# Folding w3 with w_out as plain fp32 products instead of three products of high and low parts

## The chip, the core and the metric

The kernel runs on one core of a Trainium2 chip. The metric is the device time of one execution in microseconds (us); lower is better. The time of the kernel before is 1035.65 us, the median of three runs (1032.55 to 1035.98).

## What is computed

Attention with a memory term over 4 batches of 8 heads, 576 tokens and 64 dimensions, then two feed-forward blocks over the 2304 tokens:

```python
x = attention(q, k, v, M_prev, z_prev, beta)    # (2304, 512)
a = x @ w1                                      # (2304, 1024)
b = x @ w2
h = a * b @ w3                                  # w3: (1024, 1024)
x = h @ w_out                                   # w_out: (1024, 512)
h = x @ w_in                                    # (2304, 2048)
out = (h - tanh(h)) @ w_out2                    # (2304, 512)
```

The weights of both feed-forward blocks arrive as 64-bit floats. Nothing stands between w3 and w_out, so the kernel multiplies the two once (the fold) and uses the product WF = w3 @ w_out, 1024 by 512.

## The kernel before, in words

**Stages.** Attention runs first, as 80 units (16 pairs of heads, five blocks of queries each); beside it, as background, the weights are decoded and folded. Then come six groups of 384 tokens through the first block (`ab` and `x` products), then six through the second (`h` and `o`).

**A unit of attention.** TensorE computes scores for two heads (`sc`), VectorE takes the negated maximum (L337), ScalarE the exponential with its sum (L346), VectorE the reciprocal of the sum (L355, L356), GpSimd multiplies (L363), TensorE transposes (`t`, L395 to L406), ScalarE or VectorE copies (L374, L376), and in two units of five TensorE forms the product with v (`o<-g,v`). The scores and these products are plain fp32 matmuls.

**Decoding.** A `Decoder` turns 64-bit tiles of 128 x 512 into fp32 in steps, handed out one at a time. `dec_ops` is one tile: an absolute value on ScalarE (L74) and a clamp on VectorE (L75), step one; a shift (L77), step two; the low bits (L81), step three; the sign (L84), step four. With `whole` the last writes its result into the place that `dst()` names and ends there. Without it there is a step five: GpSimd copies the result into an fp32r tile, the high part (L96), and subtracts that from the result, the low part (L99). A product of two such pairs is three fp32r matmuls: high by high, high by low, low by high.

**The fold.** `fold_work` decodes 8 tiles of w_out (`FO`, into the places z0 to z3, wa0, wb0, wa1, wb1 that later hold other weights) and 16 of w3 (`zs`; eight column blocks f, two halves of the contraction), one tile in work at a time (DW = 1), three loads ahead. After each w3 tile it issues the matmuls of that f and half, four blocks of three, into a PSUM tile `fo`; the first half is copied to a partial sum (L254), the second added to it (L257) and split into WF's high and low part (L259, L260).

**Pacing.** The background is a generator. ST = 8 steps of it are taken before the first unit. After each unit `BG` (units below MB = 40) or `BG2` (from 40 on) is added to a credit, and each whole credit takes one step; a block of fold matmuls takes none. Behind the fold the background does one group of the memory term (17 steps) and decodes four weight tiles of the first block (NE = 4), at three steps a round, 51 in all; what is left when the 80 units end is run at once. Within these bounds the compiler's scheduler orders each engine's instructions. SP's queue carries all loads.

Of the kernel before, what the change touches and what calls it, by code (L numbers as in the profile page):

```python
# [11 lines left out]
F32 = mybir.dt.float32  # L12
F32R = mybir.dt.float32r
BF16 = mybir.dt.bfloat16
U32 = mybir.dt.uint32
# [17 lines left out]
def block_kernel(ctx, tc, qk, qt, vt, mp, zp_d, beta, w1, w2, w3t, wo, wi, wo2, ident_d, mask_d, out):  # L33
# [8 lines left out]
    zp = ctx.enter_context(tc.tile_pool(name="zp", bufs=1, side="right"))  # L42
# [12 lines left out]
    def wslot(pool, tag, dt=F32R):  # L55
        return pool.tile([128, 2, 512], dt, tag=tag, name=tag if dt == F32R else tag + "p")
# [85 lines left out]
    def mm(o, lhsT, rhs, start, stop):  # L142
        return PE.matmul(o, lhsT, rhs, start=start, stop=stop).ins  # L143
# [14 lines left out]
    DW = 1  # L158
# [5 lines left out]
    OP, FL = 5, "V"  # L164
    SN, XP, MR = 2, (), 0
    TH = (("V", 0), ("A", 0))
    NE, EM, BG = 4, 1, 2.13
    BG2, MB = 2.09, 40
    MS, FS, FS5 = 4, 3, 6
    CPA = (0, 1, 3, 4)  # L170

# [6 lines left out]
    ap1, ap2, apr, ap3, ap4 = [apl[x] for x in "12r34"]  # L178
# [20 lines left out]
    def slot(tag, dt=F32R):  # L199
        return wslot(wl[0] if tag in ("wa7", "wb7") else zp if tag[0] == "z" else wfp if tag[:2] == "wf" else wp if int(tag[2]) < NE // 2 else wq[0], tag, dt)  # L200
# [4 lines left out]
    otags = ztags[:4] + etags[:4]  # L205
    FO, fv = {}, {}

    def fold_o_item(j):
        def dst():
            FO[j] = slot(otags[j])  # L210
            return FO[j][:, 0], FO[j][:, 1]

        return wo[j * 128:j * 128 + 128], dst

    def fold_item(f, half):
        def dst():
            t = wslot(ap1, "zs")
            fv[f, half] = t
            return t[:, 0], t[:, 1]

        r = slice(512 * half, 512 * half + 512)
        return w3t[r, f * 128:f * 128 + 128].rearrange("(k p) c -> p k c", p=128), dst

    def fold_work(psum):
        seq = [("o", j) for j in range(4)]
        for f in range(8):
            if f >= OP:
                seq += [("o", 4 + f - OP)] if 4 + f - OP < 8 else []
            seq.append((f, 0))
        seq += [("o", j) for j in range(12 - OP, 8)]  # L230
        for f in range(8):
            seq += [("x", i) for i, x in enumerate(XP) if x == f]
            seq.append((f, 1))
        make = {"o": fold_o_item, "x": lambda i: w_items[i]}
        dec = Decoder([make[k[0]](k[1]) if k[0] in make else fold_item(*k) for k in seq], DW, 3)
        part = {}
        for half in range(2):
            for f in range(8):
                while dec.done <= seq.index((f, half)) or half and dec.done <= seq.index(("o", 7)):
                    dec.step()  # L240
                    yield
                acc = psum()
                t = fv.pop((f, half))
                for j in range(4):
                    o = FO[4 * half + j]
                    c = slice(128 * j, 128 * j + 128)
                    mm(acc, t[:, 0, c], o[:, 0], j == 0, False)
                    mm(acc, t[:, 0, c], o[:, 1], False, False)
                    mm(acc, t[:, 1, c], o[:, 0], False, j == 3)
                    if j % FG == FG - 1:  # L250
                        yield 1
                if half == 0:
                    part[f] = wslot(wfp, f"wf{f}", F32)
                    AC.activation(out=part[f][:, 0], in_=acc, func=AF.Copy)  # L254
                else:
                    s = ap1.tile([128, 512], F32, tag=f"s{f % SN}", name="s")
                    DV.tensor_tensor(out=s, in0=acc, in1=part[f][:, 0], op=ALU.add)  # L257
                    WF[f] = wslot(wfp, f"wf{f}")
                    AC.activation(out=WF[f][:, 0], in_=s, func=AF.Copy)  # L259
                    (DV if FL == "V" else PO).tensor_tensor(out=WF[f][:, 1], in0=s, in1=WF[f][:, 0].bitcast(F32),  # L260
                                                            op=ALU.subtract)
                    yield 2

    if True:
# [271 lines left out]
        def early():  # L536
            a, b, end = None, chain(*[mem_group(g) for g in range(EM)]), object()
            ps["t"] = lambda: psT.tile([128, 512], F32, tag="t", name="mt")
            ps["o"] = lambda: psA.tile([128, 512], F32, tag="o", name="mo")
            for x in fold_work(lambda: psA.tile([128, 512], F32, tag="o", name="fo")):  # L540
                if x == 2:
                    if not mem_t:
                        mem_setup()
                    for _ in range(MR):
                        if b and next(b, end) is end:
                            b = None
                        yield
                else:
                    yield x
            if not mem_t:  # L550
                mem_setup()
            a = early_w()
            while a or b:
                if b and next(b, end) is end:
                    b = None
                yield
                for _ in range(2):
                    if a and next(a, end) is end:
                        a = None
                    yield  # L560
# [69 lines left out]
        def ab_pe(xl, f):  # L630
            o = []
            for W in (W1, W2):
                p = psb.tile([128, 512], F32, tag="ab", name="ab")
                for k in range(4):
                    c = slice(k * 128, k * 128 + 128)
                    mm(p[:, 0:N], W[f][:, 0, c], xl[0][:, k], k == 0, False)
                    mm(p[:, 0:N], W[f][:, 0, c], xl[1][:, k], False, False)
                    mm(p[:, 0:N], W[f][:, 1, c], xl[0][:, k], False, k == 3)
                o.append(p)
            return o  # L640
# [104 lines left out]
        for g in range(6):  # L745
            for f in range(8):
                wd.until(2 * f + 2)
                o = ab_pe(xl, f)
# [169 lines left out]
def build(nc, arrays):  # L918
    args = []
    for name, a in arrays.items():  # L920
        args.append(nc.dram_tensor(f"in_{name}", a.shape, mybir.dt.from_np(a.dtype), kind="ExternalInput").ap())
    o = nc.dram_tensor("out_0", (_N, 512), F32, kind="ExternalOutput").ap()
    with tile.TileContext(nc, schedule_with_timeline_sim=True) as tc:
        block_kernel(tc, *args, o)
# [40 lines left out]
```

## Time and profile before

| | |
|---|---|
| median of three runs | 1035.65 us (1032.55 to 1035.98) |
| profiled execution, its own time | 1031.13 us |
| its span | 1029.3 us |
| TensorE busy over the span | 982.1 us, 95% |
| VectorE | 752.1 us, 73% |
| ScalarE | 592.9 us, 58% |
| GpSimd | 360.5 us, 35% |
| mean granted TensorE clock | 0.991 |

PE is TensorE's matmul side, PEld its weight loads, DVE VectorE, ACT ScalarE, POOL GpSimd, SP SyncE. A line such as L143 can be a helper's (all matmuls have that one), so they are told apart by their tiles: `fo<-z,zs` is written to `fo` from `z` and `zs`. Matmuls are pipelined and their ends are modelled: records that follow one another overlap, and the spacing of their starts tells more than their length.

### The profile page before, as it was taken

Reading aid. Unit: us, or ns where it says so; the run is one execution under the profiler, and the core shown is the slowest. Engines: PE = TensorE matmul, PEld = TensorE weight load, DVE = VectorE, ACT = ScalarE, POOL = GpSimd, SP = SyncE. Lnnn points to the kernel's source line nnn. Section 1 sums busy time; section 2 is a strip of 40 time slices with the busy share of each in tenths; the row PEclk is TensorE's granted clock in tenths of the full one; section 3 lists DMA queues with packets and bytes.
Section 4 is the critical chain, followed back from the end, with each engine's and each line's share of the span. In section 5 each row is a group of like instructions: output and inputs, shape, how many; then the busy total and the mean of one; then the engine's idle time right before and its main releaser. Section 6 shows DMA issues by size and latency. Waiting matters only on the chain.

```text
span 1029.3 us, 15588 instructions
## 1 busy us (share of the span) xinstructions
PE 982.1 (95%) x5512; PEld 824.8 (80%) x5512; DVE 752.1 (73%) x1361; ACT 592.9 (58%) x1356; POOL 360.5 (35%) x396
## 2 busy tenths in 40 slices
PE   4999999889998988999999999999999999999998
PEld 2565566545787878999999998999999999989996
DVE  5858787787599986566222698778787787788875
ACT  4767766577432433333222448777786677777765
POOL 3656655585456202200000583222222222222221
PEclk9999999999999999999999999999999999999999
DMA  6434543242144552143000010000000000000000
GB/s 211 155 114 129 177 139 98 84 157 89 42 133 150 159 184 82 42 123 123 1 1 1 22 42 1 1 1 32 1 32 1 1 32 1 32 1 1 32 1 31
DMA packets 44237, 68.27 MB, mean 66 GB/s; under 512 B 4864, under 2 KB 30208, under 8 KB 44160
## 3 DMA queue, kind: packets, MB, share of 16 engines
q1 hardware_dynamic: 44160, 67.29, 20.6%
q8 instruction: 43, 0.70, 0.3%
q14 instruction: 34, 0.28, 0.1%
HBM read 62.56 MB, written 4.72 MB: 65 GB/s over the span
## 4 chain that ended last, share of the span: by engine, by line
PE 75%; DVE 14%; DMA 3%; issue 3%; ACT 2%; POOL 2%; SPq 0%; DVEq 0%; ACTq 0%; POOLq 0%
PE o L143 24%; PE h L143 19%; PE ab L143 12%; PE sc L143 6%; PE x L143 6%; PE fo L143 4%; PE t L395 3%; DVE T L81 2%; DVE T L75 2%; DVE st L337 1%; DVE T L84 1%; DVE T L77 1%; DMA mw<-in_qt 1%; ACT p L346 1%; DMA raw<-in_wi 1%
## 5 line engine op out<-in xcount | busy, mean ns | idle before, releaser
L852 POOL TENSOR_TENSOR gl<-s,gh 128x384 fp32r<-128x384 f32 x96 | 100.0, 1042 | 295.4 <-ACT gh L846 282.1
L363 POOL TENSOR_SCALAR p<-p,st 128x128 f32<-128x128 f32 (+2 forms) x144 | 94.4, 669 | 63.3 <-DVE st L356 28.7
L143 PE MATMUL x<-abh,wf 128*128 128x384 f32 x384 | 106.8, 341 | 7.3 <-ACT abh L650 7.3
L143 PE MATMUL ab<-xh,wa 128*128 128x384 f32 x384 | 110.0, 345 | 3.0 <-DVE xs L523 2.0
L143 PE MATMUL ab<-xh,wb 128*128 128x384 f32 x384 | 108.1, 340 | 1.7 <-POOL wb L96 1.7
L828 DVE SCALAR_TENSOR_TENSOR s<-s,u 128x384 f32<-128x384 f32 x96 | 84.5, 881 | 22.8 <-ACT s L818 21.6
L143 PE MATMUL sc<-r 64*64 64x288 f32 (+4 forms) x384 | 79.9, 482 | 17.0 <-ACT p L346 7.1
L346 ACT ACTIVATE p<-sc,st 128x128 f32<-128x128 f32 (+2 forms) x144 | 78.3, 549 | 29.8 <-DVE st L337 25.4
L74 ACT ACTIVATE T<-raw 128x512 f32<-128x512 f32 x72 | 48.4, 672 | 68.0 <-DMA raw<-in_wi 14.7
L824 ACT ACTIVATE u<-u,pc 128x384 f32<-128x384 f32 x96 | 59.4, 619 | 46.9 <-DVE s L828 46.9
L337 DVE TENSOR_REDUCE st<-sc 128x2 f32<-128x256 f32 (+4 forms) x80 | 64.1, 803 | 26.8 <-PE sc L143 26.3
L647 DVE TENSOR_TENSOR a<-ab,a 128x384 f32<-128x384 f32 x48 | 26.5, 551 | 74.1 <-PE ab L143 68.3
L143 PEld LDWEIGHTS x<-abh,wf 128*128 128x128 f32 x384 | 70.7, 189 | 9.4 <-ACT abh L650 9.1
L834 DVE TENSOR_TENSOR t<-h,t 128x384 f32<-128x384 f32 x96 | 53.2, 555 | 32.6 <-ACT t L817 32.2
L143 PEld LDWEIGHTS ab<-xh,wa 128*128 128x128 f32 x384 | 71.3, 190 | 6.8 <-DVE xs L523 3.1
L816 ACT ACTIVATE u<-h 128x384 f32<-128x384 f32 x96 | 47.0, 490 | 48.7 <-PE h L143 48.7
L143 PEld LDWEIGHTS ab<-xh,wb 128*128 128x128 f32 x384 | 71.1, 190 | 2.6 <-POOL wb L96 2.0
L833 DVE SCALAR_TENSOR_TENSOR s<-s,s 128x384 f32<-128x384 f32 x96 | 62.1, 647 | 8.3
L143 PE MATMUL x<-abl,wf 128*128 128x384 f32 x192 | 66.1, 344 | 1.6 <-DVE abl L651 1.6
L143 PE MATMUL ab<-xl,wa 128*128 128x384 f32 x192 | 65.6, 342 | 0.0
L143 PE MATMUL ab<-xl,wb 128*128 128x384 f32 x192 | 65.2, 340 | 0.0
L840 DVE COPY_PREDICATED s<-u,t 128x384 f32<-128x384 uint32 x96 | 58.7, 612 | 8.7
(214 smaller groups left out, 2578.6 us busy)
## 6 DMA issues: line engine op xcount, KB each, us to landing
raw<-in_wo SPq DMA_DIRECT2D x24, 512.0 KB, 3.6
r<-in_qk SPq DMA_DIRECT2D x15, 576.0 KB, 4.6
raw<-in_w3t SPq DMA_DIRECT2D x16, 512.0 KB, 3.7
raw<-in_w SPq DMA_DIRECT2D x16, 512.0 KB, 3.7
raw<-in_wi SPq DMA_DIRECT2D x16, 512.0 KB, 3.8
v<-in_vt SPq DMA_DIRECT2D x16, 320.0 KB, 3.9
mw<-in_qt SPq DMA_DIRECT2D x18, 256.0 KB, 2.9
out<-ob SPq DMA_DIRECT2D x18, 256.0 KB, 2.3
```

The costliest lines, as they stand in the source:

```text
L74: AC.activation(out=tf, in_=hw.bitcast(F32), func=AF.Abs)
L143: return PE.matmul(o, lhsT, rhs, start=start, stop=stop).ins
L337: mark["V"][n] = DV.tensor_reduce(out=st[:, 0:2] if u < 4 else st[:, 0:1], in_=seen(n), axis=AX.X if u < 4 else AX.XY, op=ALU.max, negate= ...
L346: mark["A"][n] = AC.activation(out=p[:, x], in_=sc[:, x], func=AF.Exp, bias=st[:, x.start:x.start + 1], accum_out=st[:, 2 + x.start:3 + x. ...
L363: (DV if NV[u] == "V" else PO).tensor_scalar(out=pr, in0=pr, scalar1=sc, scalar2=1.0, op0=ALU.mult, op1=ALU.mult)
L816: AC.activation(out=u, in_=o, func=AF.Square)
L824: AC.activation(out=u, in_=u, func=AF.Relu, bias=pc[:, 2:3])
L828: DV.scalar_tensor_tensor(out=s1, in0=s1, scalar=k2[0], in1=u, op0=ALU.add, op1=ALU.mult)
L833: DV.scalar_tensor_tensor(out=s1, in0=s2, scalar=k2[1], in1=s1, op0=ALU.add, op1=ALU.mult)
L834: DV.tensor_tensor(out=t, in0=o, in1=t, op=ALU.subtract)
L840: DV.copy_predicated(out=s1, mask=u[:].bitcast(U32), data=t)
L852: PO.tensor_tensor(out=l, in0=s1, in1=h[:].bitcast(F32), op=ALU.subtract)
```

## The change

The decoder of the fold is made with `whole=True`: each tile of w_out and w3 stays one fp32 tile, and each block of the fold is one plain fp32 matmul. The w3 tiles move from a pool with one buffer, which held both parts, to one with two, half as large each; the w_out tiles keep their places and use the first half of them. The two pacing constants go to 1.84. Everything behind the fold, WF's two parts among it, stays as it is.

```diff
-    NE, EM, BG = 4, 1, 2.13
-    BG2, MB = 2.09, 40
+    NE, EM, BG = 4, 1, 1.84
+    BG2, MB = 1.84, 40
...
     def fold_o_item(j):
         def dst():
-            FO[j] = slot(otags[j])
-            return FO[j][:, 0], FO[j][:, 1]
+            if j < 4:
+                FO[j] = wslot(zp, otags[j], F32)[:, 0]
+            else:
+                FO[j] = slot(otags[j], F32)[:, 0]
+            return FO[j].bitcast(U32)
...
     def fold_item(f, half):
         def dst():
-            t = wslot(ap1, "zs")
-            fv[f, half] = t
-            return t[:, 0], t[:, 1]
+            t = fv[f, half] = ap2.tile([128, 512], F32, tag="zs", name="zs")
+            return t[:].bitcast(U32)
...
-        dec = Decoder([make[k[0]](k[1]) if k[0] in make else fold_item(*k) for k in seq], DW, 3)
+        dec = Decoder([make[k[0]](k[1]) if k[0] in make else fold_item(*k) for k in seq], DW, 3, whole=True)
...
-                    mm(acc, t[:, 0, c], o[:, 0], j == 0, False)
-                    mm(acc, t[:, 0, c], o[:, 1], False, False)
-                    mm(acc, t[:, 1, c], o[:, 0], False, j == 3)
+                    mm(acc, t[:, c], o, j == 0, j == 3)
```

## Rows read from the trace of the kernel before

**Rows 1.** The page, part 1: busy us (share of the span) and instructions

```profile
PE 982.1 (95%) x5512; PEld 824.8 (80%) x5512; DVE 752.1 (73%) x1361; ACT 592.9 (58%) x1356; POOL 360.5 (35%) x396
```

**Rows 2.** Busy time by stretch: start-up, fold, rest of attention

```profile
core 0: us, PE busy (x) PEld busy (x) DVE busy (x) ACT busy (x) POOL busy (x), PEclk, DMA share, GB/s
0.00:34.00 34.00, 20.29 (x105) 9.83 (x105) 21.67 (x50) 18.53 (x52) 16.92 (x29) 0.95 0.61 203
34.00:198.00 164.00, 162.11 (x1037) 98.17 (x1035) 122.09 (x266) 111.68 (x307) 97.11 (x129) 1.00 0.41 127
198.00:262.00 64.00, 54.74 (x397) 29.87 (x397) 50.22 (x120) 45.31 (x130) 41.39 (x57) 0.97 0.36 114
```

**Rows 3.** The chain of waits, 34 to 198 us: its shares by line

```profile
by line: PE sc L143 27.9%; PE fo L143 27.0%; PE o L143 17.4%; PE t L395 14.2%; DMA r<-in_qk 2.9%; ACT p L346 2.7%; DVE st L337 2.7%; PE t L402 1.1%; DVE wf L260 1.0%; issue 0.8%; DVE st L355 0.7%; ACT r L194 0.4%; DVE T L81 0.4%; DVE g L376
```

**Rows 4.** The chain of waits, 0 to 34 us: its shares by line

```profile
by line: DMA raw<-in_wo 17.2%; issue 12.6%; POOL p L363 8.7%; DVE st L337 8.3%; PE sc L143 6.2%; PE o L143 6.2%; DVE T L81 5.7%; DVE T L75 5.1%; DVE T L84 4.5%; SPq L186 3.8%; ACT T L74 3.6%; POOL z L99 2.6%; ACT p L346 2.3%; PE t L402 1.9%
```

**Rows 5.** Instructions of tile fo: ns min/median/max, first to last start, form

```profile
L143 PEld LDWEIGHTS fo<-z,zs x96: 186/188/192, 38.1 to 122.8; 128*128 128x128 f32 x96
L143 PE MATMUL fo<-z,zs x96: 390/397/500, 38.1 to 123.0; 128*128 128x512 f32 x96
...
L143 PE MATMUL fo<-wa,zs x48: 387/394/505, 135.1 to 193.1; 128*128 128x512 f32 x48
```

**Rows 6.** Timeline of TensorE, 101 to 109 us: start, us, instruction

```profile
100.62 0.40 PE L143 MATMUL sc<-r 64*64 64x288 f32 x1
...
102.32 0.69 PE L143 MATMUL sc<-r 64*64 64x288 f32 x2
...
105.22 3.08 PE L143 MATMUL fo<-z,zs 128*128 128x512 f32 x12
108.13 0.27 PE L395 MATMUL t<-ident,p 128*128 128x128 f32 x1
```

**Rows 7.** Timeline of TensorE, 139.7 to 146 us

```profile
139.81 0.92 PE L143 MATMUL sc<-r 64*128 64x384 f32 x4
...
144.25 1.13 PE L143 MATMUL sc<-r 64*128 64x512 f32 x4
145.31 0.28 PE L143 MATMUL sc<-maskb,identb 128*128 128x128 bf16 x2
```

**Rows 8.** Groups of GpSimd, 34 to 198 us: busy us, mean ns, idle before

```profile
L99 POOL TENSOR_TENSOR zs<-T,zs 128x512 fp32r<-128x512 f32 x16 | 20.3, 1271 | 0.9
L96 POOL TENSOR_SCALAR zs<-T 128x512 fp32r<-128x512 f32 x16 | 9.9, 618 | 12.1 <-PE fo L143 5.0 <-DVE T L84 4.2 <-DVE st L356 2.9
```

**Rows 9.** Groups of GpSimd, 0 to 34 us

```profile
L99 POOL TENSOR_TENSOR z<-T,z 128x512 fp32r<-128x512 f32 x4 | 5.6, 1396 | 0.2
L96 POOL TENSOR_SCALAR z<-T 128x512 fp32r<-128x512 f32 x4 | 3.0, 746 | 15.1 <-DVE st L356 13.1 <-DVE st L355 2.0
```

**Rows 10.** Groups of VectorE, 34 to 198 us: the decode steps

```profile
L84 DVE SCALAR_TENSOR_TENSOR T<-raw,T 128x512 uint32<-128x512 uint32 x20 | 14.4, 721 | 0.1
L77 DVE TENSOR_SCALAR T<-T 128x512 uint32<-128x512 uint32 x21 | 12.1, 574 | 0.3
L75 DVE TENSOR_SCALAR T<-T 128x512 f32<-128x512 f32 x21 | 10.7, 507 | 2.1 <-ACT T L74 1.7
```

**Rows 11.** One line's instructions, L75 and L77, 0 to 200 us: ns min/median/max

```profile
L75 DVE TENSOR_SCALAR T<-T x26: 400/427/1342, 10.3 to 191.9; 128x512 f32<-128x512 f32 x26
...
L77 DVE TENSOR_SCALAR T<-T x26: 403/428/1370, 11.5 to 192.4; 128x512 uint32<-128x512 uint32 x26
```

**Rows 12.** Timeline of VectorE, 18 to 21 us

```profile
18.40 0.88 DVE L75 TENSOR_SCALAR T<-T 128x512 f32<-128x512 f32 x1 [0.18 <-ACT T L74]
19.31 1.37 DVE L77 TENSOR_SCALAR T<-T 128x512 uint32<-128x512 uint32 x1
```

**Rows 13.** Waits, 34 to 198 us: who for whom, total us, times, longest

```profile
DVE s L257 <- PE fo L143: 7.4, 5, 2.0
```

## The prediction, made before the changed kernel was run

> **What bounds the kernel now.** I read four views, from wide to narrow. First the page: TensorE is busy for 95% of the span, GpSimd for 35% [rows 1]. An average says nothing about one stage, so next the table of stretches [rows 2]. The fold lies in the second of its rows, 34 to 198 us, beside attention: there TensorE is busy 162.1 of 164 us at a granted clock of 1.00 (the 2.4 GHz level), VectorE 122, ScalarE 112, GpSimd 97. Before it, in the start-up, TensorE works 20.3 of 34 us; behind it, 198 to 262 us, 54.7 of 64. Third, the chain of waits: over the fold's stretch the scores, the fold, the products with v and the transposes hold 87.6% of it (27.9 + 27.0 + 17.4 + 14.2 + 1.1), all on TensorE [rows 3]; over the start-up no engine leads, and GpSimd has 11.3%, the decode steps of VectorE (L81, L75, L84) 15.3% [rows 4]. Fourth, the instructions. So in the fold's stretch a microsecond put on TensorE is a microsecond on the end, and one taken from GpSimd is worth nothing by itself; only in the start-up and in the stretch behind the fold could other engines give something back.
>
> **The products.** Removed: 192 fp32r matmuls of 512 columns (96, and two rows of 48, of which one stands) [rows 5]. A group of twelve, for one f and one half, starts at 105.22 and the next instruction at 108.13: 2.91 us, or 0.235 each with some 0.09 for getting in [rows 6]. Sixteen groups: 46.6 us.
>
> Added: 64 plain fp32 matmuls of the same shape. No row has that shape in fp32, so its price is built from others. An fp32 matmul of this kernel leaves two records: the scores of 512 columns are two matmuls a unit, one for each head, and stand there as x4 [rows 7]. The two heads use different rows of the array and overlap, so such a group is two passes deep. From 384 to 512 columns it grows from 0.92 to 1.13 us: 0.21 us for 128 columns in each of two passes, 0.82 ns a column, two clocks at 2.4 GHz (0.83). That the heads really overlap is seen where two records of 288 columns stand alone: together 0.69 us, of which the last takes 0.40, so one starts 0.29 behind the other [rows 6], where one clock a column would give 0.12. A 512-column pass then takes 0.427 us and a matmul 0.85; four matmuls with 0.09 to get in are 3.50 us, sixteen groups 56.1. **TensorE gains 56.1 − 46.6 = +9.5 us**, in a stretch where it has 1.9 us idle. Ends: the scores of 512 columns, 144.25 to 145.31, spend 0.53 a pass, as if each weight load were exposed [rows 7]: sixteen times 8 × 0.53 + 0.09 is 69.3, +22.7. At the other end a pass of one clock a column, as fp32r has, would make −18.0 (16 × (8 × 0.213 + 0.09) = 28.6). I take 0.427, since here the passes follow one another on the full array like the fp32r ones, whose loads of 0.188 us [rows 5] fit into a 0.235 slot and fit better into a 0.427 one.
>
> Here a rule of the Trainium skill speaks the other way: Perfetto Trace Analysis, Engine Utilization, notes the array's output rate as divided by two for FP32_LOW_HIGH. By it a 512-column fp32 matmul would take an estimated 0.43 us in all and the sum would be −18.0; the unpaired rows above, at twice that for each of two records, do not agree, and it is kept as a rival.
>
> **The decode.** Removed from GpSimd: 24 copies (L96) and 24 subtractions (L99), for the sixteen w3 items 9.9 + 20.3 us [rows 8], for the eight w_out items a like price, with 3.0 + 5.6 us of it in the start-up [rows 9]. In the fold's stretch that is hidden twice: GpSimd is idle 67 of 164 us [rows 2], and TensorE is the later one. VectorE keeps its four operations an item; the last now writes the product's operand itself. GpSimd's work also stretches VectorE's: the median of L75 and L77 is 0.43 us, their mean in this stretch 0.51 and 0.57 [rows 10, 11]; 0.23 us an item, 4.5 us over 20 items, can come back. It is worth nothing while TensorE covers it, 4.5 if that cover is gone. The Trainium skill's GPSIMD Engine Reference, Specifications, says that the two engines share SBUF interfaces; the rows agree (0.57 us where the median is 0.43).
>
> **Start-up.** Here the relief counts. L99 is 2.6% of the chain, 0.9 us [rows 4]; L75 and L77 at 18.4 us take 0.88 and 1.37 [rows 12] against 0.43, 1.4 us. Against it: the eight steps that run ahead of the main loop now hold two whole items, with one more L84 (0.72) before the first maxima. Net −1.6; I take −1.5. Ends: −3.8 (all of GpSimd's 11.3% of 34 us) and +0.7.
>
> **Pacing.** An item is four steps where it was five, so the fold is 96 steps for 120. Eight run ahead. Before, 40 units at 2.13 and 12.8 at 2.09 finish it at unit 52.8; after, 88 at 1.84 finish it at 47.8. The 51 steps that follow (one memory group, four weight items) end at unit 77.2 before, 75.5 after, of 80: nothing spills. Behind the fold a unit takes 64 / 27.2 = 2.35 us, TensorE 2.01 of it; five more units there bring 5 × 0.34 = +1.7 us of idle time, while the background gets thinner (1.84 for 2.09 a unit) and shortens that idle by something unknown. I take 0, between +1.7 and −9.3, the whole idle time of that stretch [rows 2], nearer the first because the chain of one unit (maximum, exponential, norm) stays as it is.
>
> **Buffers and queues.** The w3 tile goes from one two-part buffer to two whole ones, the same bytes. The wait for the fold's matmuls, 5.0 us in 6 places on GpSimd [rows 8], moves to L84 on VectorE, with the next maxima and sums queued behind it and ScalarE's exponentials waiting for those. It needs matmuls a whole item older than before, so I cost it at nothing; uncovered it is up to 5.0. The evacuation (L257) waits for a longer group: it waited 7.4 us in 5 places [rows 13], and each group ends 0.6 us later, which TensorE's other work covers. DMAs, SP's queue and the instructions behind attention stay the same, merely later.
>
> **Sum:** +9.5 − 1.5 + 0 = +8.0 us. The profiled execution took 1031.13 (span 1029.3), so 1039.1 there; it lies 4.5 under the median of the runs, 1035.65, to which the forecast is tied: **1043.6**.
>
> **Rivals.**
> 1. *The new wait bites* (slower): L84 stands on VectorE for all 5.0 us: 1048.6. For: TensorE is saturated, so its queue lags. Against: one more buffer. 0.10.
> 2. *Exposed weight loads* (slower): each fp32 pass costs 0.53, +22.7 − 1.5: 1056.9. For: the 512-column scores. Against: they load half the rows behind a change of tile shape; the fold's own loads hide. 0.07.
> 3. *Relief pays* (not slower): the path runs through VectorE and GpSimd between TensorE's instructions, and the 4.5 us of stretched decode plus 3.8 in the start-up come off against +9.5: 1036.9; with 6 of the 9.3 us idle behind the fold 1030.9. It decides only where TensorE's queue runs dry, and in the fold's stretch that is 1.9 us. 0.07 for no change, 0.05 for faster.
> 4. *One clock a column* (faster): −18.0 − 1.5: 1016. Only if the paired records hide a serial order; the unpaired ones speak against it. 0.04. The footnote of the Trainium skill's Perfetto Trace Analysis named above says this of fp32.
> 5. *It does nothing*: the longer products fill time that busy TensorE only seems to use, since ends of matmuls are modelled, and the start-up's 1.5 is left: 1034.2. For: the chain has 12% off TensorE. 0.05.
>
> **How the numbers follow.** The forecast has 0.62, between 1039 and 1048 by the ends of its small terms. A measurement here can tell 0.3%, 3.1 us. Slower: 0.62 + 0.10 + 0.07 = 0.79; within 0.3%: 0.07 + 0.05 = 0.12; faster: 0.05 + 0.04 = 0.09. The range takes in the forecast, the new wait, no change and the relief's near case, 1033.5 to 1050; outside are exposed loads, one clock a column and the relief's far case, 0.16.
>
> **What would show it.** In the changed profile the fold's matmuls should be 128 records, spaced about 0.43 us within a group, a group 3.5; the stretch that holds the fold should show TensorE near 100% busy and take with the next stretch some 9 us more; attention should end about 8 us later and all behind it keep its length. GpSimd should fall by about 46 us without effect. A spacing near 0.53 or 0.21, long waits of VectorE for the fold at L84, or an attention that ends no later would each prove a step wrong.

## The result, and the profile after

The changed kernel took 1044.76 us (median of 4 runs, 1042.59 to 1047.67) against 1034.1 for the kernel before on the same chip: a ratio of 1.0114 with a 95% interval of [1.0093, 1.0135]: slower by some 1.1%. The forecast was 1043.6, within 1033.5 to 1050. The profiled execution took 1046.89 us, its span 1044.8.

The first part of the page of the changed kernel, as in [rows 1]:

```profile
PE 991.4 (95%) x5448; PEld 816.8 (78%) x5448; DVE 742.5 (71%) x1361; ACT 593.3 (57%) x1356; POOL 314.4 (30%) x348
```

Read against [rows 1], this row splits the longer span in two. TensorE works 9.3 us more (991.4 − 982.1), where the products were forecast to add 9.5. But the span grew by 15.5 us (1029.3 to 1044.8), so TensorE is also idle 6.2 us longer, and the forecast has no term for that. GpSimd lost 46.1 us and 48 instructions, as forecast, and the matmul records fell by 64, 192 less 128.

The 9.3 is not the products alone. These are the stretches up to the first product behind attention, before and then after:

```profile
0.00:265.70 265.70, 240.84 (x1560) 139.72 (x1560) 197.50 (x440) 178.32 (x495) 156.69 (x215) 0.99 0.42 132
0.00:272.80 272.80, 244.40 (x1484) 125.90 (x1485) 190.38 (x443) 177.01 (x492) 106.01 (x167) 1.00 0.41 129
```

Up to there TensorE works only 3.6 us more; the other 5.7 lie behind it, where a stretch of lower clock is shown below. So the whole-span figure comes near 9.5 in part by chance, and the price of the products has to be read from the products themselves.

The stretches of [rows 2] in the changed kernel, same columns:

```profile
0.00:34.00 34.00, 20.60 (x124) 10.19 (x125) 23.27 (x57) 21.12 (x59) 10.05 (x23) 1.00 0.65 218
34.00:198.00 164.00, 158.19 (x879) 79.54 (x879) 106.01 (x244) 100.04 (x274) 50.40 (x80) 1.00 0.38 119
198.00:262.00 64.00, 56.67 (x423) 31.40 (x419) 52.96 (x125) 49.19 (x143) 40.03 (x58) 1.00 0.39 123
```

In the fold's stretch TensorE is busy 158.2 of 164 us where it was busy 162.1: each fold product costs it more, and yet it waits more. The next stretch has less idle time than before (7.3 us for 9.3).

TensorE's timeline around one group of the fold (start, us, instruction):

```profile
111.32 1.08 PE L143 MATMUL fo<-z0p,zs 128*128 128x512 f32 x2
112.24 1.02 PE L143 MATMUL fo<-z1p,zs 128*128 128x512 f32 x2
113.10 1.02 PE L143 MATMUL fo<-z2p,zs 128*128 128x512 f32 x2
113.95 1.02 PE L143 MATMUL fo<-z3p,zs 128*128 128x512 f32 x2
114.91 0.70 PE L143 MATMUL sc<-r 64*128 64x256 f32 x4
```

Each matmul is two records, and the next begins 0.85 or 0.86 us later (112.24, 113.10, 113.95): 0.43 a pass (one of the two records), as forecast. The group takes 3.59 us from its first start to the next instruction, for 3.50 forecast and 2.91 before [rows 6].

The waits of the fold's stretch (who for whom: total us, times, longest), three rows of the changed kernel and one of the kernel before:

```profile
DVE s L257 <- PE fo L143: 5.5, 6, 2.6
PE sc L143 <- ACT p L346: 4.6, 6, 1.5
DVE zs L84 <- PE fo L143: 2.7, 2, 1.5
```

```profile
PE sc L143 <- ACT p L346: 1.8, 5, 0.8
```

The evacuation at L257 waits 5.5 us for 7.4 [rows 13]. The third row is the wait that was to move from GpSimd to VectorE at L84, where it was costed at nothing: it is there, 2.7 us in two places. The second row is what saturated TensorE had little of before: the scores wait for ScalarE's exponentials, 4.6 us for 1.8.

VectorE's decode steps there (busy us, mean ns, idle before), for [rows 10]:

```profile
L77 DVE TENSOR_SCALAR T<-T 128x512 uint32<-128x512 uint32 x20 | 10.4, 519 | 0.3
L75 DVE TENSOR_SCALAR T<-T 128x512 f32<-128x512 f32 x20 | 8.6, 429 | 2.4 <-ACT T L74 2.2
```

L75 came down to its undisturbed 0.43 us; L77 about a third of the way, 574 to 519 ns.

Next I set landmarks in the traces: the first and last product of the fold, and the first matmul of the stage behind attention (tile ab), in us. The last four columns are of experiments told below: the changed kernel once more, the products alone, the changed kernel with one pair of instructions turned back, and the same with a third buffer.

| | before | after | after, repeated | products alone | pair turned back | with third buffer |
|---|---|---|---|---|---|---|
| first fold product | 38.1 | 36.4 | 36.8 | 39.4 | 37.6 | 36.8 |
| last fold product | 193.8 | 193.7 | 193.6 | 205.9 | 195.0 | 194.1 |
| first product ab | 265.7 | 272.8 | 274.5 | 275.6 | 275.0 | 271.6 |

Attention ends 7.1 us later, near the forecast 8. But the span grew by 15.5, so about as much again is lost behind it, where "all behind it keep its length" was forecast. There one row stands out, GpSimd's multiply L502, which before has 1037/1044/1487 ns (least, median, most). Changed kernel:

```profile
L502 POOL TENSOR_TENSOR mw<-mw,mst x18: 1033/1044/5666, 206.4 to 452.3; 128x512 f32<-128x512 f32 x18
```

One of its 18 executions takes 5.67 us. The timeline of VectorE, GpSimd and TensorE around it (in brackets: how long the engine stood idle before, and for whom):

```profile
345.45 0.54 DVE L647 TENSOR_TENSOR a<-ab,a 128x384 f32<-128x384 f32 x1
345.92 0.15 DVE L500 TENSOR_TENSOR mst<-mst,gates 128x8 f32<-128x8 f32 x1
346.00 0.41 DVE L77 TENSOR_SCALAR T<-T 128x512 uint32<-128x512 uint32 x1
...
350.24 0.67 DVE L84 SCALAR_TENSOR_TENSOR z6p<-raw,T 128x512 uint32<-128x512 uint32 x1
...
346.15 5.67 POOL L502 TENSOR_TENSOR mw<-mw,mst 128x512 f32<-128x512 f32 x1 [4.03 <-DVE mst L500]
351.87 1.12 PE L506 MATMUL mo<-ident,mw 128*128 128x128 f32 x4 [3.90 <-POOL mw L502]
```

The same place in the kernel before:

```profile
336.94 0.16 DVE L500 TENSOR_TENSOR mst<-mst,gates 128x8 f32<-128x8 f32 x1
337.07 0.56 DVE L647 TENSOR_TENSOR a<-ab,a 128x384 f32<-128x384 f32 x1
337.54 1.30 DVE L77 TENSOR_SCALAR T<-T 128x512 uint32<-128x512 uint32 x2
...
337.18 1.04 POOL L502 TENSOR_TENSOR mw<-mw,mst 128x512 f32<-128x512 f32 x1 [3.55 <-DVE mst L500]
```

L500 and L647 have changed places on VectorE's queue. Before, L500 releases L502 while L647 runs, whose operand ab lies in PSUM, and L502 takes 1.04 us. After, L500 is followed by an unbroken row of VectorE instructions on SBUF operands until 350.91, and L502 ends at 351.82, 0.9 us behind it. TensorE's mo product needs L502 and waits 3.90 us for it. The 22 us that follow L500, in the changed kernel and then before:

```profile
346.00:368.00 22.00, 17.09 (x80) 14.35 (x81) 15.12 (x32) 6.80 (x15) 8.35 (x3) 0.84 0.36 121
```

```profile
337.00:359.00 22.00, 20.52 (x116) 17.46 (x115) 21.97 (x47) 9.79 (x21) 4.77 (x5) 0.99 0.52 159
```

TensorE is busy 3.4 us less there, VectorE 6.9 us less, and the granted clock is down, 0.84 for 0.99 over the stretch. So two losses without a term in the forecast are suspected: VectorE's wait at L84, and the multiply at L502. The experiments test both, apart from the products.

### The profile page after: what moved, and what is told of

Read it like the earlier page. It is cut to its first block, busy times and chain, and to the rows that moved or that the text cites. A ratio compares the mean times of both kernels' runs of the same rounds, so it can differ in the third digit from the quotient of the medians.

```text
span 1044.8 us, 15433 instructions
## 1 busy us (share of the span) xinstructions
PE 991.4 (95%) x5448; PEld 816.8 (78%) x5448; DVE 742.5 (71%) x1361; ACT 593.3 (57%) x1356; POOL 314.4 (30%) x348
## 4 chain that ended last, share of the span: by engine, by line
PE 57%; DVE 5%; issue 2%; DMA 1%; POOL 1%; ACT 0%; SPq 0%; DVEq 0%; POOLq 0%; ACTq 0%
PE h L143 19%; PE o L143 19%; PE ab L143 12%; PE x L143 6%; DVE T L81 1%; PE mo L143 1%; DVE T L77 1%; DVE T L75 1%; DMA raw<-in_wo 0%; DVE abl L651 0%; PE mo L506 0%; DVE T L84 0%; DVE a L647 0%; DVE wa L710 0%; DMA mc<-in_zp 0%
## 5 line engine op out<-in xcount | busy, mean ns | idle before, releaser
L363 POOL TENSOR_SCALAR p<-p,st 128x128 f32<-128x128 f32 (+2 forms) x144 | 89.8, 636 | 148.5 <-DVE st L356 68.7
L143 PE MATMUL sc<-r 64*64 64x288 f32 (+4 forms) x384 | 75.6, 474 | 21.4 <-ACT p L346 15.3
L647 DVE TENSOR_TENSOR a<-ab,a 128x384 f32<-128x384 f32 x48 | 26.4, 551 | 75.2 <-PE ab L143 70.7
L650 ACT ACTIVATE abh<-a 128x384 fp32r<-128x384 f32 x48 | 25.0, 522 | 76.3 <-DVE a L647 76.2
```

The source lines that it names most:

```text
L363: (DV if NV[u] == "V" else PO).tensor_scalar(out=pr, in0=pr, scalar1=sc, scalar2=1.0, op0=ALU.mult, op1=ALU.mult)
```

## The experiments

Ratios are to the kernel before on the same chip: one chip for the first four experiments, another for the next four, a third for the last two.

**The change again, and the products alone.** The first is the changed kernel unedited. The second is the kernel before with its decode and pacing, and only the products exchanged:

```
-                    mm(acc, t[:, 0, c], o[:, 0], j == 0, False)
-                    mm(acc, t[:, 0, c], o[:, 1], False, False)
-                    mm(acc, t[:, 1, c], o[:, 0], False, j == 3)
+                    mm(acc, t[:, 0, c].bitcast(F32), o[:, 0].bitcast(F32), j == 0, j == 3)
```

> The changed kernel itself, profiled once more. The profiled execution of the changed kernel (1046.89 us) was 7.6 us late at the end of attention and 15 us late from 360 us on; in between one GpSimd multiply of a memory token (L502, at 346 us) took 5.67 us instead of 1.04. If that is an accident of single executions (theory), other executions of the same program lack it: with 1042 to 1043 us the L502 at that place takes 1.0 to 1.5 us and attention still ends 7 to 9 us later than before. If it belongs to the changed program (rival), every execution has it, and it is part of the price of the change: then the profile shows it again at 5 to 6 us.

> The kernel before with one edit: the three fp32r products of each block become one plain fp32 product of the two high parts. Decoder, GpSimd's copies and subtractions, buffers and pacing stay as before; left out are the low parts in the products. Theory (TensorE's passes are the whole price): 64 x 0.854 us for 192 x 0.235, +9.5 us, so 1043 to 1045 where before has 1034 to 1035. Rival (the loss comes from the new pacing, buffers or wait for L84, not from the passes): within 3 us of before.

The repeat: 1047.0 us, 1.0134 [1.0105, 1.0162], with the same stall (L502 at most 5.660 us). So the stall is no accident of one execution. But one of the six took 1038.1, and two of the first four 1042.6; both profiles are of executions near 1047, and whether the faster ones stall isn't known.

The products alone: 1039.19 us (1037.82 to 1041.84), 1.0071 [1.0053, 1.0089], some 7.3 us, less than the 9.5 expected. Its fold's stretch, drawn to its later end at 206:

```profile
34.00:206.00 172.00, 170.31 (x959) 85.67 (x957) 123.59 (x265) 111.59 (x308) 95.21 (x129) 1.00 0.38 122
```

TensorE is 99% busy (170.31 of 172) and the fold ends 12.1 us later. So with the decode as it was, TensorE stays saturated, the price of the products goes nearly whole to the end of attention (+9.9, in a profile of the slowest of its five executions, 1041.84) and mostly to the end; there is no stall at the multiply (at most 1.51 us). The rest of the loss came with the other parts of the change.

**The decode and pacing, with products at the old price.** In the changed kernel each product becomes three bf16 products of the upper 16 bits of both operands, or, in the second, one:

```
-                    mm(acc, t[:, c], o, j == 0, j == 3)
+                    tb, ob = [z.bitcast(BF16).rearrange("p (n t) -> p n t", t=2)[:, :, 1] for z in (t[:, c], o)]
+                    for i in range(3):
+                        mm(acc, tb, ob, j == 0 and i == 0, j == 3 and i == 2)
```

> The changed kernel with each fp32 product replaced by three bf16 products of the upper 16 bits of the same tiles (a column a clock, so that TensorE pays about what it paid before: some 0.22 to 0.24 us each, 192 of them); whole decoding, GpSimd without the fold's copies and subtractions, the new buffers and the pacing of 1.84 stay. Left out: the fold's product is not the sum of high and low parts. This shows what the relief of GpSimd is worth by itself. Theory: 1 to 4 us under before (start-up alone), 1031 to 1034. Rival (relief of VectorE and GpSimd pays along the whole fold): 6 us or more under before, 1028 or less. Rival (new pacing or buffers cost time): above before.

> The same with one bf16 product for each block instead of three: TensorE loses 128 x 0.23 = 29 us of work against the kernel with three. If TensorE's queue sets the pace of the fold's stretch (theory), most of it comes off until another engine leads: a unit of attention without fold takes 2.35 us where TensorE has 2.01, so over some 43 units beside the fold, 3.1 us each now, at most 0.75 us a unit, and I expect 18 to 29 us under the kernel with three products. Rival (the products only fill time that other engines leave): under 8 us.

With three, 1033.68 us (12 runs, 1026.09 to 1037.93), 1.0017 [0.9997, 1.0037]. A bf16 product is spaced 0.226 us, so its 192 are some 2 us cheaper than those of before. Even so the median lies 2.3 us above before (1031.36), where 1 to 4 us under was expected: by it the decode, buffers and pacing gave nothing and may cost a few us, though single executions scatter by 12 us. Its profiled execution, the fastest, has ab begin at 260.4 and no stall; it is one of twelve and shows only that the parts can go well together. With one, 1010.44 us, 0.979 [0.9769, 0.9811], ab at 236.2: 128 products of 0.226 us, 29 us of TensorE's work, taken away give 23 of them back, stall included (5.66 us there too). So some eight tenths of the work taken from TensorE come off the time, as expected (18 to 29 us).

**The order at L500, both ways.** In the changed kernel the memory step is issued ahead of the chain that holds L647, for the one f where the two had met:

```
+                if (g, f) == (0, 7):
+                    for _ in range(MS):
+                        mem_step()
...
-                for _ in range(MS):
+                for _ in range(MS if (g, f) != (0, 7) else 0):
```

In the kernel before, the reverse: that L500 is held until L647 has been issued.

```
+            with tc.issue_after(m647[0, 7]) if (g, tl) == (2, 2) else ExitStack():
                 DV.tensor_tensor(out=st[:, 0:8], in0=st[:, 16:24], in1=gates, op=ALU.mult)
...
+            m647[g, f] = DV.tensor_tensor(out=a, in0=o[1][:, 0:N], in1=a, op=ALU.mult).ins
```

> The changed kernel with one edit: in the last step of the first group of tokens the memory steps are issued ahead of the products' evacuation. On VectorE's queue this turns round one pair at about 346 us, so that the small multiply that releases GpSimd's L502 (L500) stands before the product L647, as in the kernel before, and not behind it; up to there both queues are the same. Theory (GpSimd's L502 starves because VectorE runs one operation with two SBUF inputs after the other behind L500, and gets its turn when L647, which reads PSUM, stands there): L502 takes 1.0 to 1.5 us, TensorE's idle 3.9 us behind it and the clock's drop are gone, and the time is 1037 to 1041, 6 to 9 us under the changed kernel. Rival (the stall comes from elsewhere, as late data): L502 stays at 5 to 6 us and the time at 1045 to 1048.

> The reverse in the kernel before: L500 is issued behind L647 at that place and nothing else is changed up to there. Theory: L502 there takes over 4 us in most executions and the time goes from 1031 to 1036 to 1040. Rival: it stays at 1029 to 1034.

The timeline of the changed kernel with the pair turned back:

```profile
348.26 0.15 DVE L500 TENSOR_TENSOR mst<-mst,gates 128x8 f32<-128x8 f32 x1
348.33 0.54 DVE L647 TENSOR_TENSOR a<-ab,a 128x384 f32<-128x384 f32 x1
348.80 1.01 DVE L77 TENSOR_SCALAR T<-T 128x512 uint32<-128x512 uint32 x1
...
348.49 1.04 POOL L502 TENSOR_TENSOR mw<-mw,mst 128x512 f32<-128x512 f32 x1 [3.54 <-DVE mst L500]
349.58 0.66 PE L506 MATMUL mo<-ident,mw 128*128 128x128 f32 x4 [1.16 <-POOL mw L502]
```

The 22 us that follow L500 in it:

```profile
348.30:370.30 22.00, 19.16 (x109) 16.21 (x109) 21.93 (x48) 9.04 (x21) 4.88 (x5) 1.00 0.49 160
```

And of the kernel before with the pair exchanged:

```profile
336.90 0.55 DVE L647 TENSOR_TENSOR a<-ab,a 128x384 f32<-128x384 f32 x1
337.36 0.16 DVE L500 TENSOR_TENSOR mst<-mst,gates 128x8 f32<-128x8 f32 x1
...
341.21 0.55 DVE L651 TENSOR_TENSOR abl<-a,abh 128x384 fp32r<-128x384 f32 x1
...
337.60 5.06 POOL L502 TENSOR_TENSOR mw<-mw,mst 128x512 f32<-128x512 f32 x1 [4.03 <-DVE mst L500]
```

The order makes and unmakes the stall in both kernels: 5.67 to 1.04, and 1.04 to 5.06. That is shown. With the pair turned back TensorE's wait for the multiply falls from 3.90 to 1.16 us, and the granted clock over the 22 us is 1.00 for 0.84. The price to the end is less clear. Turned back, the changed kernel took 1041.18 us, 1.0081 [1.0067, 1.0094], some 5.5 us under the repeat by the ratios, for 6 to 9 expected. But the kernel before with the stall took 1030.9 us, 0.9986 [0.9969, 1.0002], not the 1036 to 1040 expected. Its twelve runs fall in two groups of six, 1027.4 to 1029.6 and 1032.2 to 1034.5, the profiled one (1033.97) in the upper, 2.8 us above the profiled execution of before. The edit also moved the order behind the pair (z7p's L84 then stands ahead of L490, where before it stood behind), so a run's time holds both, and what the stall alone costs stays open; it need not cost its length.

**The old pacing**, in the changed kernel:

```
-    NE, EM, BG = 4, 1, 1.84
-    BG2, MB = 1.84, 40
+    NE, EM, BG = 4, 1, 2.13
+    BG2, MB = 2.09, 40
```

> The changed kernel with the pacing constants of before (2.13 and 2.09). The fold ends some 7 units earlier and the background altogether at about unit 65. Theory (TensorE's work sets the pace, the order of it matters little): the first product behind attention starts within 3 us of the changed kernel's (272.8 to 274.5 us). Rival (the pacing is what the change lives on, or dies of): over 4 us earlier or later. The end also depends on whether L502 stalls in the new order.

It took 1047.83 us, 1.0149 [1.0134, 1.0164]. The first product behind attention starts at 277.3, 2.8 us later than in the repeat and 4.5 later than in the first profile of the changed kernel, so it settles neither the theory (within 3 us) nor the rival (over 4). L502 stalls here too, less long and at another place:

```profile
304.55 3.55 POOL L502 TENSOR_TENSOR mw<-mw,mst 128x512 f32<-128x512 f32 x1
```

So the old pace is no better than the new; what of the time is pacing and what the order behind it stays open.

Its trace bears on TensorE's idle time in the fold. From the first fold product to the last, and from there to the first product behind attention, with the old pace:

```profile
37.00:176.40 139.40, 138.46 (x730) 68.28 (x729) 95.21 (x209) 85.04 (x230) 44.21 (x65) 1.00 0.38 127
176.40:277.30 100.90, 89.06 (x613) 48.30 (x612) 74.12 (x177) 68.16 (x201) 58.17 (x80) 0.95 0.31 95
```

And with the new one, in the changed kernel:

```profile
36.40:193.70 157.30, 151.49 (x832) 76.01 (x830) 99.68 (x231) 96.27 (x264) 46.83 (x75) 1.00 0.39 120
193.70:272.80 79.10, 69.91 (x511) 38.06 (x510) 65.37 (x151) 57.66 (x166) 47.77 (x67) 1.00 0.34 105
```

With the same decode and buffers TensorE is idle 0.9 us beside the fold at the old pace, 5.8 at the new. So the idle time beside the fold isn't a matter of the decode alone. At the old pace more of it lies behind the fold instead (11.8 us for 9.2), and attention ends no earlier.

**A fold of the high parts alone**, from the kernel before: L99 left out, one fp32r product a block.

```
-            return t[:, 0], t[:, 1]
+            return t[:, 0], None
...
+                    mm(acc, t[:, 0, c], o[:, 0], j == 0, j == 3)
```

> The kernel before with the fold made of the high parts alone: one fp32r product a block, GpSimd's copy kept, its subtraction left out, pacing as before. The low parts of w3 and w_out are left out of the fold. Theory: TensorE loses 128 x 0.235 = 30 us in the fold and as with the single bf16 product 18 to 25 us come off: 1006 to 1013. Rival (GpSimd's relief and the faster pacing made part of that gain): under 15 us, 1016 or more.

It took 1004.68 us, 0.9727 [0.9711, 0.9743], ab at 238.3: 128 fp32r products of 0.235 us (30 us) less give 27.5, more than the 18 to 25 expected; GpSimd's subtractions left out may have a part in that. It is faster than both kernels, but it isn't the same fold: the low parts are left out of the product.

**A third buffer for the w3 tile**, on top of the pair turned back, beside a repeat of that kernel:

```
-            t = fv[f, half] = ap2.tile([128, 512], F32, tag="zs", name="zs")
+            t = fv[f, half] = ap1.tile([128, 512], F32, tag=f"zs{(8 * half + f) % 3}", name="zs")
```

> The changed kernel with the one pair on VectorE's queue turned round, once more, to be compared with the next on one chip: 1.007 to 1.010 of before, L502 under 1.5 us, L84's waits for the fold 2 to 3 us.

> The same with three w3 tiles instead of two (the pairs' order as in the run above). Theory (the wait for the fold's matmuls, 2.7 us in two places on VectorE at L84, holds up the maxima and exponentials behind it, and so TensorE's scores, which wait 4.6 us for ScalarE in the fold's stretch where they waited 1.8 before): L84's wait is gone, the scores' wait falls to 2 us or less, and 2 to 4 us come off. Rival (the wait is covered, the scores wait for another reason): less than 1 us of difference.

The repeat: 1042.43 us, 1.0094 [1.0076, 1.0113]; with the third buffer 1039.43 us, 1.0065 [1.0048, 1.0081]; 3.0 us less by the medians, as the wait theory had it, though the intervals overlap a little. The waits of the fold's stretch, first two buffers, then three:

```profile
DVE st L355 <- ACT p L346: 17.0, 19, 1.7
PE sc L143 <- ACT p L346: 4.7, 6, 1.4
DVE zs L84 <- PE fo L143: 2.7, 2, 1.5
```

```profile
PE sc L143 <- ACT p L346: 4.7, 7, 1.2
DVE st L355 <- ACT p L346: 10.5, 15, 1.6
```

L84's row is gone, ab begins 3.4 us earlier (271.6 for 275.0), and VectorE's waits for the exponentials fall from 17.0 to 10.5. The scores' wait for ScalarE stays at 4.7, where the theory wanted 2 or less, so it has another cause than L84.

That the 3.0 us came off through L84's wait is not shown, and the trace speaks against the direct way. These are the two waits with two buffers, and TensorE in the stretch that holds them:

```profile
41.33 0.69 DVE L84 SCALAR_TENSOR_TENSOR zs<-raw,T 128x512 uint32<-128x512 uint32 x1 [1.21 <-PE fo L143]
52.78 0.69 DVE L84 SCALAR_TENSOR_TENSOR zs<-raw,T 128x512 uint32<-128x512 uint32 x1 [1.47 <-PE fo L143]
```

```profile
38.00:76.00 38.00, 38.00 (x191) 18.36 (x189) 20.15 (x48) 22.75 (x63) 10.54 (x18) 1.00 0.34 106
```

TensorE is busy for all 38.00 us around both waits, so they cost it nothing there. At the old pace L84 waits longer, 5.3 us in three places, and TensorE is idle only 0.9 us beside the whole fold. With the third buffer the fold takes as long as with two (157.3 us from first to last product for 157.4), the fold starts 0.8 us earlier, and the other 2.5 us are gained behind its last product. The third buffer also changes the order of instructions on VectorE's, ScalarE's and TensorE's queues from the first wait on. Whether that order or a late effect of the wait gave the 3.0 us stays open.

## Why the prediction came near, and where it failed

The forecast was near, and its main term, the products, is borne out; part of the nearness is luck. On the same chip the change costs 10.7 us by the first medians, and by the repeat's ratio 13.8, where the forecast had 8.0. That the forecast lies only 1.2 us under the first median comes in part from the kernel before, which took 1034.1 there and 1035.65 when the forecast was tied to it.

The ratios can be set out as a chain that ends at the repeat's 1.0134, some 13.8 us: the products alone 7.3 (1.0071); decode and pacing, with three buffers and the old order of the pair, −0.6 (1.0065); two buffers for three +3.0 (1.0094); the pair as the changed kernel has it +4.1 (1.0134). Each step is the difference to the one before, so the sum comes out by construction. The steps lie on three chips and are good to a few us; by the first comparison (1.0114) the last would be 2.0, by the other run of the pair turned back (1.0081) 5.5.

- **Two passes of 0.427 us: right.** The median spacing is 0.429. This settles rivals 2 (0.53) and 4 (one clock a column). The Trainium skill's Perfetto Trace Analysis, Engine Utilization, has a factor of two for FP32_LOW_HIGH, from which the prediction estimated 0.43 us a matmul. The records show 0.86.
- **"TensorE gains +9.5": near for the products, not for the path.** One group measured 3.59 us for 3.50. When the products are exchanged alone, 7.3 us reach the end. In the changed kernel TensorE's busy time grew by 9.3, but only 3.6 of that up to the end of attention.
- **Start-up −1.5: about right.** The fold starts 0.5 to 1.7 us earlier in four profiles of the changed kernel and of the pair turned back, whose queues are the same up to there (36.4 to 37.6 for 38.1).
- **"Near 100% busy": wrong.** TensorE has 158.2 of 164 us, 96%, where the products with the old decode and pace had 99%. At the old pace with the new decode it is 99% again beside the fold (138.46 of 139.4), and the idle time lies behind the fold.
- **"I cost it at nothing" at L84: not refuted.** The wait came, 2.7 us in two places, against the step's argument that the matmuls would be done by then. But TensorE covered it. The third buffer's 3.0 us show that two buffers cost something, and not how. Rival 1 named this wait, at 5.0.
- **GpSimd −46 us without effect: near in part by chance.** The 46.1 hold the stall; with the pair turned back GpSimd lost 52.0 (360.5 to 308.5). L75 and L77 gave 0.13 us an item for the 0.23 reckoned, and no run shows it in the time.
- **Pacing 0: unsettled.** Old and new pace differ by less than the order behind attention moves.
- **"The instructions behind attention stay the same, merely later": wrong, the clearest miss.** They are the same, but their order on VectorE's queue is not, and one exchanged pair made L502 take 4.6 us longer (5.67 for 1.04).

So the forecast has no term for what the order behind attention and the two buffers cost, some 5 to 8 us together by the ratios above, and charges the products 2 us more than they cost at the end. The two errors offset each other in part.

## What to carry to other kernels

Where TensorE is saturated, price a change of its products from spacings in the kernel's own timeline, and take most of that (here eight to nine tenths) for the time. Then ask what keeps TensorE full. A wait that has moved onto another engine isn't yet a loss: look whether TensorE stood still beside it. And an edit that takes the wait away can change the order of every queue, so a gain doesn't prove the wait was the cause. Don't assume that code behind the change keeps its length: compare the order on each queue, and look at the longest, not the median, of every line that a shift in time can touch.

## What the hardware showed unexpectedly

One GpSimd multiply took 1.04, 5.06 or 5.67 us by what VectorE did as it became ready. In both stalls it ended 0.9 us behind the last of VectorE's unbroken row (351.82 against 350.91, 342.66 against 341.76), and so did the 3.55 us of the old pacing (308.10 against 307.20). That is nearly the length of one undisturbed execution, as if it began only there. Where it got in during L647, VectorE's L77 took 1.01 us in its stead (0.41 in the stalled kernel). The Trainium skill's SBUF — State Buffer, Who interferes with whom, says that a GpSimd instruction that reads SBUF and a VectorE one with two SBUF inputs, or a VectorE one in a two-port mode and any of GpSimd's, exclude each other for a whole instruction, by which starts first. The rows agree with that and add that the loser lost to a row of them. That it is this interface was argued from operands and ends, not shown: no run here changed an operand's place.
